# Issuing one input load from another engine's queue, and reordering the products around a weight fold

## The chip, the cores and the metric

The kernel runs on one core of one Trainium2 chip. The metric is the device time of one execution in microseconds (us), and a program's time is the median of its runs. A core has TensorE (PE, with its weight loads shown as PEld), VectorE (DVE), ScalarE (ACT), GpSimd (POOL), SyncE (SP, which here only issues DMAs) and 16 DMA engines. In this kernel TensorE's products go to PSUM, and ACT and DVE copy them from there to SBUF.

## The reference

```python
h  = x + A(layernorm(x))        # x: 2048 tokens x 640, bfloat16
h2 = h + B(layernorm(h))        # B: (gelu(x @ w_gate) * (x @ w_up)) @ w_down, 640 -> 1536 -> 640
# A: 32 heads of 20 columns
q, k, v = split(x @ wqkv)
phi(q)  = [softmax(q @ w_phi), softmax(-(q @ w_phi))]      # per head, 40 features
phi(k)  = the same of k
kv, z   = sum over tokens of phi(k) outer v,  sum of phi(k)
A(x)    = (phi(q) @ kv) / (phi(q) . z + 1e-6) @ wo
```

The attention is linear, so keys and values of all 2048 tokens must have been reduced to `kv` before any query can be finished.

## The kernel before, in words

Tokens are worked on in 16 tiles of 128 (`t` = 0 to 15), 640 columns each; the 640 rows of a weight are 5 blocks of 128 (`c`, or `d` for the blocks that a fold makes). `x_sb[b]` holds four tiles of x.

**Stages.** First each tile is normalized, transposed into `LN1T`, and multiplied by `Wv` (a v product, 10 matmuls of 320 columns) and by the folded key weight `Wk2` (a k product, also 10). This stage is what the change touches. After it come the queries (`q_mm`), attention, and the feed-forward block with the long `gate_up` and `down` products.

**The fold.** `w_phi` is applied to the key weight and not to the keys. For each block `d`, `fold(WkT, Wk2, False, (d,))` (L232) multiplies the transposed block `WkT[:, :, d]` by a block-diagonal matrix `BD`: 6 matmuls into a PSUM tile `wa`, which is then copied to `Wk2[:, d]`. Blocks 0, 1, 3 and 4 are copied by ACT (L257), block 2 by DVE (L259). `WkT` comes from HBM as five transposing DMAs, one for each `d`, issued by SP at L203 ahead of everything that SP issues later. A k product of block `c` needs `Wk2[:, c]`, so `k_part(t, c, ...)` (L326) can do some blocks of a tile before the other folds are made; `k_tile(t)` (L331) adds block 4 where a tile was begun that way (tiles 0 and 1), and runs the two exponentials on ACT (L340).

**PSUM.** All products share four PSUM tiles (`gtile`, L111, and the transposes' `tp`, L162), given out in rotation: a product can begin when the tile given out four places earlier has been read by ACT or DVE. So the order of calls also sets who waits for which copy.

**Order.** Nothing is reordered by a scheduler: each engine runs its instructions in the order of the program text. The text between L439 and L489 is an order written by hand, with halves of v products (`v_part`, L306), statistics (`ln_st`, L275, on DVE, with its `between` call inside), normalizations (`ln_ap`, L279), TensorE transposes (`ln_tp`, L286) and copies of v (`v_ev`, L315, on ACT). From tile 4 on the normalized tiles are transposed by DMAs that SP issues (L167).

**Loads of x.** Tiles 0 to 5 are loaded by SP at L189 to L198, ahead of the transposes of `WkT`. Tiles 6 and 7 are loaded by SP at L470, behind these transposes in SP's order, and read first by the statistics of L488. A DMA issue uses one of eight semaphores in rotation, and waits until the load eight issues earlier has landed; for L470 that is the load of tile 3 (L196). The one load that ACT issues before the change is that of `w_phi` (L191).

Of the kernel before, what the change touches and what calls it, by code (L numbers as in the profile page):

```python
# [17 lines left out]
def kernel(  # L18
# [12 lines left out]
    nc = tc.nc  # L31
# [41 lines left out]
    x_v = A_x.rearrange("b (p t) d -> p (b t) d", t=NT)  # L73
# [11 lines left out]
    x_sb = [const.tile([P, 4, D], BF16, name=f"x_sb{b}") for b in range(NB)]  # L85
# [25 lines left out]
    def gtile(name):  # L111
        return psG.tile([P, 2, 512], F32, name=name, tag="G")
# [46 lines left out]
    def transpose_to(dst, src, on_pe, on_dve=False):  # L159

        if on_pe:
            tp = psG.tile([P, 16, P], BF16, name="tp", tag="G")  # L162
            for c in range(NC):
                nc.tensor.transpose(tp[:, c, :], src[:, c * P:(c + 1) * P], ident)  # L164
            (nc.vector.tensor_copy if on_dve else nc.scalar.copy)(dst, tp[:, 0:NC, :])  # L165
        else:
            nc.sync.dma_start_transpose(dst, src)  # L167
# [9 lines left out]
    Wk2 = p1.tile([P, NC, D], BF16, name="Wk2")  # L177
# [5 lines left out]
    WkT = fp.tile([P, NC, D], BF16, name="WkT")  # L183
# [42 lines left out]
    def warm(*cols):  # L226
        for n in cols:
            nc.tensor.matmul(wu[:, 0, 0:n], lhsT=ones[:, 0:P], rhs=ones[:, 0:n], start=True, stop=True)
# [3 lines left out]
    def fold(WT, W2, quarters, ds=range(NC)):  # L232


        n, w = 1, HD
        runs = []
        for c in range(NC):
            lo, hi = H0[c] * Dh, (H0[c] + NH[c]) * Dh
            for r in range(2 * n):
                a, b = max(lo, r * w), min(hi, (r + 1) * w)  # L240
                if a < b:
                    runs.append((r // n, r, c, a, b))
        runs.sort()
        for d in ds:
            wa = gtile("wa")
            wr = wa.rearrange("p u (q x) -> p (u q) x", q=n)
            for i, (u, r, c, a, b) in enumerate(runs):
                nc.tensor.matmul(wr[:, r, a - r * w:b - r * w], lhsT=WT[:, c, d * P:(d + 1) * P],  # L248
                                 rhs=BD[:, c].rearrange("p a b -> p (a b)")[:, a - H0[c] * Dh:b - H0[c] * Dh],
                                 start=(i == 0 or runs[i - 1][0] != u),  # L250
                                 stop=(i + 1 == len(runs) or runs[i + 1][0] != u), skip_group_check=True)
            dst, src = W2[:, d, :].rearrange("p (u f) -> p u f", u=2), wr[:, :, 0:w]
            if quarters:
                dst = W2[:, d, :].rearrange("p (c u m f) -> p u m c f", c=NC, u=2, m=2)
                src = src.rearrange("p u (m c f) -> p u m c f", m=2, c=NC)
            if d in (QA if quarters else KA):
                nc.scalar.copy(dst, src)  # L257
            else:
                nc.vector.tensor_copy(dst, src)  # L259
# [19 lines left out]
    def ln_ap(t, on_act=False, on_pe=False):  # L279
        ln = (ln_act if on_act else ln_dve)(p1, "1", *lnp[t])  # L280
        if on_pe:
            lnp[t] = ln
        else:
            transpose_to(LN1T[t // 4][:, :, t % 4 * P:(t % 4 + 1) * P], ln, False)

    def ln_tp(t, on_dve=False):  # L286
        transpose_to(LN1T[t // 4][:, :, t % 4 * P:(t % 4 + 1) * P], lnp[t], True, on_dve)
# [5 lines left out]
    def proj(ps, t, W, us=(0, 1), cs=None):  # L293
        order = [(u, c) for u in us for c in range(NC)] if cs is None else [(u, c) for c in cs for u in us]
        for u, c in order:
            nc.tensor.matmul(ps[:, u, 0:HD], lhsT=lnT(t, c), rhs=W[:, c, u * HD:(u + 1) * HD],  # L296
                             start=(c == 0), stop=(c == NC - 1))
# [3 lines left out]
    def v_mm(t, us=(0, 1)):  # L301
        if 0 in us:
            pv[t] = gtile("pv")
        proj(pv[t], t, Wv, us)

    def v_part(t, *cs):  # L306

        if 0 in cs:
            pv[t] = gtile("pv")
        for c in cs:  # L310
            for u in range(2):
                nc.tensor.matmul(pv[t][:, u, 0:HD], lhsT=lnT(t, c), rhs=Wv[:, c, u * HD:(u + 1) * HD],  # L312
                                 start=(c == 0), stop=(c == NC - 1))

    def v_ev(t):  # L315
        nc.scalar.activation(vS[t % NV][:, :, 1:VC].rearrange("p (u h) f -> p u h f", u=2),
                             pv[t][:, :, 0:HD].rearrange("p u (h f) -> p u h f", f=Dh), ACTF.Copy,
                             scale=lnp[t][2] if t in CT else 1.0)
# [7 lines left out]
    def k_part(t, *cs):  # L326
        if 0 in cs:
            pks[t] = gtile("pk")
        proj(pks[t], t, Wk2, cs=cs)

    def k_tile(t):  # L331
        if t in pks:
            pk = pks[t]
            k_part(t, NC - 1)
        else:
            pk = gtile("pk")
            proj(pk, t, Wk2)
        Ek[t] = ev.tile([P, 2, D], BF16, name="E", bufs=10)
        for s in range(2):
            nc.scalar.activation(Ek[t][:, s, :].rearrange("p (u f) -> p u f", u=2), pk[:, :, 0:HD],  # L340
                                 ACTF.Exp, scale=((lnp[t][2], nrstd[t]) if t in CT else (1.0, -1.0))[s])
# [61 lines left out]
    def st_act(t, i):  # L403

        xt, v = x_sb[0][:, t, :], va[t]
        if i == 0:
            nc.scalar.activation(sqa, xt, ACTF.Identity, scale=-1.0 / D, accum_out=v[:, 0:1])
        else:
            nc.scalar.activation(sqa, xt, ACTF.Square, bias=v[:, 0:1], accum_out=v[:, 1:2])
            nc.gpsimd.tensor_scalar(v[:, 2:3], v[:, 1:2], 1.0 / D, EPS, op0=ALU.mult, op1=ALU.add)  # L410
            nc.gpsimd.tensor_tensor(v[:, 3:4], v[:, 2:3], nhalf[:, 0:1], op=ALU.pow)
            nc.gpsimd.tensor_scalar(nrstd[t], v[:, 3:4], -1.0, None, op0=ALU.mult)
            lnp[t] = xt, None, v[:, 3:4], None
# [16 lines left out]
    def bd(c0, c1):  # L430

        n = c1 - c0
        nc.vector.tensor_tensor(BD[:, c0:c1], wphi[:, c0:c1, None, :].to_broadcast([P, n, 8, Dh]),
                                hmask[:, c0:c1, :, None].to_broadcast([P, n, 8, Dh]), ALU.mult)
# [9 lines left out]
    ln_st(2, act=False, log=True)  # L444
    bd(0, NC)
    st_act(1, 1)
    warm(*[P] * 4)
    v_part(0, 0, 1)
    v_part(1, 0, 1)
# [17 lines left out]
                                op0=ALU.mult, op1=ALU.add)  # L467
    ln_st(4, act=False, between=lambda: ln_ap(3, on_pe=True))
    ln_tp(3, True)
    nc.sync.dma_start(x_sb[1][:, 2:4, :], x_v[:, 6:8, :])  # L470
    v_ev(2)
    fold(WkT, Wk2, False, (0,))
    fold(WkT, Wk2, False, (1,))
    ln_st(5, act=False, between=lambda: ln_ap(4))
    nc.sync.dma_start(x_sb[2][:, 0:2, :], x_v[:, 8:10, :])
    fold(WkT, Wk2, False, (2,))
    v_mm(3)
    v_ev(3)
    fold(WkT, Wk2, False, (3,))
    k_part(0, 0, 1, 2)  # L480
    k_part(1, 0)
    fold(WkT, Wk2, False, (4,))
    k_part(1, 1, 2)
    k_part(0, 3)
    k_part(1, 3)
    ln_ap(5)
    nc.sync.dma_start(x_sb[2][:, 2:4, :], x_v[:, 10:12, :])
    ln_st(6)  # L488
# [5 lines left out]
    for t in range(NT):  # L494
        if t == T3:
            kvp = gtile("kvp")[:, 0, 0:2 * QF].rearrange("p (s f) -> p s f", s=2)
        late = t in (1, 2, 3, 4)
        if 0 < t < NT - 6 and not late:
            ln_ap(t + 6, on_act=True)
        k_tile(t)  # L500
        if t == 0:
            ln_ap(6)
            nc.sync.dma_start(x_sb[3][:, 0:2, :], x_v[:, 12:14, :])
        if t in FQ:
            fold(WqT, Wq2, True, [i for i, f in enumerate(FQ) if f == t])
        for i in KVG.get(t, ()):
            kv_tile(i)
        for j in range(len(QT)):
            if t == QT[j]:
                q_mm(j)  # L510
                q_exp(j)
                if j == 0:
                    nc.gpsimd.tensor_copy(Wg[:, 0, 0:1], Eq[j][:, 0, 1, 0:1])
                for i in KVQ.get(j, ()):
                    kv_tile(i)
        if 0 < t < NT - 3:
            v_mm(t + 3)
        if late:
            ln_ap(t + 6, on_act=True)
        if t == 1:  # L520
            nc.sync.dma_start(x_sb[3][:, 2:4, :], x_v[:, 14:16, :])
        if 0 < t < NT - 3:
            v_ev(t + 3)
        for i in ST.get(t, ()):
            ln_st(i, i + 1)
        k_norm(t)
        load_T(WqT, 0, *[i for i, f in enumerate(LQ) if f == t])
        if t == 10:
            transpose_to(LN1T[0][:, :, P:2 * P], ln_a(1), False)
        if t == 13:  # L530
            ln_ap(0, on_act=True)
        if t == 8:
            for z in KT:
                nc.gpsimd.memset(z, 0.0)
        if t == 5:
            nc.sync.dma_start(Wo, wo_v)
# [401 lines left out]
```

## Time and profile before

| what | value |
|---|---|
| runs before | 271.77, 272.64, 272.80 us; median 272.64 |
| the profiled execution | 272.35 us |
| its span, first to last instruction | 270.6 us, so 1.75 us lie around it |
| TensorE busy | 266.1 us, 98% of the span |
| VectorE, ScalarE, GpSimd busy | 173.9, 138.6, 101.2 us |
| granted TensorE clock | 1.0 |
| HBM traffic | 47 GB/s over the span |

Times of instructions count from the start of the span. A matmul's row gives its start and the modelled time until its result is out; matmuls are pipelined, so ten of 320 columns that start 0.136 us apart take 1.36 us of TensorE's time although their row says 1.52. A bracket at the end of a row of the timeline is the idle time of the engine before it, and what ended it. The row of a DMA issue tells how long the issuing engine was at it; the landing of its data is another number.

### The profile page before, as it was taken

How to read it: one execution, taken by the hardware profiler on the slowest of the kernel's cores; microseconds unless marked ns; L12 is line 12 of the kernel's file. 1: busy time of each engine (PE TensorE's matmuls, PEld its weight loads, DVE VectorE, ACT ScalarE, POOL GpSimd, SP SyncE). 2: the span in 40 equal slices, each digit the busy share in tenths (PEclk: the TensorE clock that was granted, in tenths of full speed). 3: DMA queues.
4: the chain of work that ended last, by engine and by line, in shares of the span. 5: the costliest groups of instructions: out<-in, count | busy, mean ns of one | idle time of the engine just before them, and what ended most of it. 6: DMA issues, size and time to landing. Idle time of an engine off the chain costs nothing.

```text
span 270.6 us, 7029 instructions
## 1 busy us (share of the span) xinstructions
PE 266.1 (98%) x2857; PEld 172.0 (64%) x2857; DVE 173.9 (64%) x347; ACT 138.6 (51%) x249; POOL 101.2 (37%) x238
## 2 busy tenths in 40 slices
PE   8999999999999999999999999999999999999995
PEld 6777777765455887788755455775555476444574
DVE  5789999996877767876566783568673332333322
ACT  5779997877789675245541356421544300322100
POOL 5448898887002335376211564014661100000000
DMA  6987489213864442432301222203222101000011
GB/s 187 206 199 169 81 210 96 46 37 85 326 201 112 157 101 55 68 78 50 51 27 51 48 50 48 50 3 75 76 46 51 24 24 51 24 0 0 4 48 48
DMA packets 45264, 22.10 MB, mean 82 GB/s; under 512 B 37808, under 2 KB 43184, under 8 KB 45232
## 3 DMA queue, kind: packets, MB, share of 16 engines
q1 hardware_dynamic: 44576, 21.64, 33.5%
q8 instruction: 22, 0.36, 0.6%
q10 hardware_dynamic: 656, 0.03, 0.2%
q14 instruction: 10, 0.08, 0.1%
HBM read 10.18 MB, written 2.62 MB: 47 GB/s over the span
## 4 chain that ended last, share of the span: by engine, by line
PE 96%; DMA 2%; SPq 0%; DVE 0%; issue 0%
PE gu L768 39%; PE pd L790 19%; PE pq L396 8%; PE pk L296 8%; PE po L708 8%; PE pv L296 7%; DMA Wv<-in_A_wqkv_dram 2%; PE kvp L374 2%; PE pv L312 2%; PE ab L619 1%; PE wa L248 1%; PE ab L586 1%; PE tp L164 0%; SPq L193 0%; SPq L190 0%; SPq L189 0%
## 5 line engine op out<-in xcount | busy, mean ns | idle before, releaser
L771 ACT ACTIVATE g<-gu 128x512 bf16<-128x512 f32 (+1 forms) x60 | 30.4, 510 | 74.0 <-PE gu L768 73.2
L774 DVE TENSOR_TENSOR GT<-gu,g 128x512 bf16<-128x512 f32 (+1 forms) x60 | 34.3, 579 | 46.8 <-PE gu L768 38.6
L768 PE MATMUL gu<-LN2T,Wg 128*128 128x512 bf16 (+1 forms) x300 | 61.8, 337 | 0.0
L768 PE MATMUL gu<-LN2T,Wu 128*128 128x512 bf16 (+1 forms) x300 | 61.8, 336 | 0.0
L790 PE MATMUL pd<-Wd,GT 128*128 128x320 bf16 (+4 forms) x396 | 53.9, 295 | 0.0
L790 PEld LDWEIGHTS <-GT 128*128 128x128 bf16 x396 | 37.6, 98 | 14.5 <-DVE GT L774 0.2
L768 PEld LDWEIGHTS <-Wu 128*128 128x128 bf16 x300 | 29.4, 98 | 22.6
L768 PEld LDWEIGHTS <-Wg 128*128 128x128 bf16 x300 | 29.1, 98 | 21.2
L296 PEld LDWEIGHTS <-LN1T 128*128 128x128 bf16 x290 | 28.0, 98 | 10.4
L355 POOL TENSOR_TENSOR E<-E,rs 128x640 bf16<-128x640 bf16 x25 | 31.7, 1295 | 4.4 <-DVE rs L351 2.8
L792 DVE TENSOR_TENSOR y<-pd,x_sb 128x320 bf16<-128x320 f32 (+4 forms) x33 | 15.8, 480 | 24.1 <-PE pd L790 24.1
L708 PE MATMUL po<-Wo,oT 128*128 128x320 bf16 x160 | 24.5, 299 | 0.0
L296 PE MATMUL pk<-Wk,LN1T 128*128 128x320 bf16 x160 | 24.4, 299 | 0.0
L396 PE MATMUL pq<-LN1T,Wq 128*128 128x512 bf16 x100 | 22.9, 379 | 0.0
L347 DVE TENSOR_REDUCE sk<-E 128x64 f32<-128x1280 bf16 x16 | 22.9, 1430 | 0.0
L401 ACT ACTIVATE Eq<-pq 128x1024 bf16<-128x1024 f32 (+1 forms) x26 | 19.9, 831 | 2.8 <-PE pq L396 2.7
L340 ACT ACTIVATE E<-pk 128x640 bf16<-128x640 f32 x28 | 19.1, 769 | 3.0 <-PE pk L296 3.0
L708 PEld LDWEIGHTS <-oT 128*128 128x128 bf16 x160 | 15.6, 98 | 7.3 <-ACT oT L165 0.2
L296 PE MATMUL pv<-Wv,LN1T 128*128 128x320 bf16 x130 | 19.8, 299 | 0.0
L151 ACT ACTIVATE ln<-x_sb,v,rstd 128x640 bf16<-128x640 bf16 x14 | 12.9, 920 | 13.0 <-POOL v L747 12.9
L396 PEld LDWEIGHTS <-Wq 128*128 128x128 bf16 x100 | 9.4, 98 | 10.3
L683 DVE TENSOR_TENSOR tt<-AB,w 128x1280 bf16<-128x1280 f32 x10 | 15.1, 1505 | 0.4 <-POOL w L676 0.3
(120 smaller groups left out, 291.4 us busy)
## 6 DMA issues: line engine op xcount, KB each, us to landing
out_dram<-y SPq DMA_DIRECT2D x15, 160.0 KB, 1.8
x_sb<-in_A_x_dram SPq DMA_DIRECT2D x6, 320.0 KB, 3.3
Wd<-in_B_w_down_dram SPq DMA_DIRECT2D x1, 1440.0 KB, 6.8
Wg<-in_B_w_gate_dram SPq DMA_DIRECT2D x1, 1152.0 KB, 7.3
Wu<-in_B_w_up_dram SPq DMA_DIRECT2D x1, 1152.0 KB, 5.6
Wo<-in_A_wo_dram SPq DMA_DIRECT2D x1, 800.0 KB, 5.0
Wg<-in_B_w_gate_dram SPq DMA_DIRECT2D x1, 768.0 KB
Wu<-in_B_w_up_dram SPq DMA_DIRECT2D x1, 768.0 KB, 9.1
```

What stands on the lines that cost most here:

```text
L296: nc.tensor.matmul(ps[:, u, 0:HD], lhsT=lnT(t, c), rhs=W[:, c, u * HD:(u + 1) * HD], start=(c == 0), stop=(c == NC - 1))
L340: nc.scalar.activation(Ek[t][:, s, :].rearrange("p (u f) -> p u f", u=2), pk[:, :, 0:HD], ACTF.Exp, scale=((lnp[t][2], nrstd[t]) if t in C ...
L347: nc.vector.reduce_sum(sk, Ek[t].rearrange("p s (h f) -> p (s h) f", f=Dh), axis=AX.X)
L355: eng.tensor_tensor(e, e, rs[:, s * H:(s + 1) * H, None].to_broadcast([P, H, Dh]), ALU.mult)
L396: nc.tensor.matmul(pqs[j][:, i, :], lhsT=Wq2[:, kc, c * P:(c + 1) * P], rhs=LN1T[b][:, kc, :], start=(kc == 0), stop=(kc == NC - 1))
L401: nc.scalar.activation(Eq[j][:, :, s, :], pqs[j][:, 0:len(QG[j])], ACTF.Exp, scale=(1.0, -1.0)[s])
L708: nc.tensor.matmul(pos[u], lhsT=st[t][:, c, :], rhs=Wo[:, c, u * HD:(u + 1) * HD], start=(c == 0), stop=(c == NC - 1))
L768: nc.tensor.matmul(gu[i][:, 0:n], lhsT=W[:, c, f * P:(f + 1) * P], rhs=LN2T[b][:, c, a0:a1], start=(c == 0), stop=(c == NC - 1))
L771: nc.scalar.activation(g[:, 0:n], gu[0][:, 0:n], ACTF.Gelu_apprx_tanh)
L774: nc.vector.tensor_tensor(st[b, "g", f][:, a0:a1], gu[1][:, 0:n], g[:, 0:n], ALU.mult)
L790: nc.tensor.matmul(pd[:, 0:f1 - f0], lhsT=st[b, "g", f][:, tl * P:(tl + 1) * P], rhs=Wd[:, f, f0:f1], start=(f == 0), stop=(f == NF - 1), ...
L792: nc.vector.tensor_tensor(y[:, f0:f1], pd[:, 0:f1 - f0], x_sb[b][:, tl, f0:f1], ALU.add)
```

## The change

The load of x tiles 6 and 7 is taken from SP (L470) and given to ACT, in the text right after the second half of tile 1's statistics (L446). SP has one load less between the transposes of `WkT` and the first transpose of a normalized tile.

The other edits change the order of TensorE's work, with the copies that belong to it:

- the fold of block 2 moves from before the v product of tile 3 to after it;
- ahead of the fold of block 4 there is only block 0 of tile 0's k product and block 0 of tile 1's (before: blocks 0, 1, 2 of tile 0 and block 0 of tile 1);
- after that fold, tile 0's blocks 1, 2, 3 and (in `k_tile`) 4 are done together, and tile 1's blocks 1, 2, 3 follow after tile 0's `k_tile`, ahead of tile 1's.

No matmul, copy or load is added or taken away.

```diff
     bd(0, NC)
     st_act(1, 1)
+    nc.scalar.dma_start(x_sb[1][:, 2:4, :], x_v[:, 6:8, :])
     warm(*[P] * 4)
...
     ln_tp(3, True)
-    nc.sync.dma_start(x_sb[1][:, 2:4, :], x_v[:, 6:8, :])
     v_ev(2)
     fold(WkT, Wk2, False, (0,))
     fold(WkT, Wk2, False, (1,))
     ln_st(5, act=False, between=lambda: ln_ap(4))
     nc.sync.dma_start(x_sb[2][:, 0:2, :], x_v[:, 8:10, :])
-    fold(WkT, Wk2, False, (2,))
     v_mm(3)
     v_ev(3)
+    fold(WkT, Wk2, False, (2,))
     fold(WkT, Wk2, False, (3,))
-    k_part(0, 0, 1, 2)
+    k_part(0, 0)
     k_part(1, 0)
     fold(WkT, Wk2, False, (4,))
-    k_part(1, 1, 2)
-    k_part(0, 3)
-    k_part(1, 3)
+    k_part(0, 1, 2, 3)
     ln_ap(5)
...
         k_tile(t)
         if t == 0:
+            k_part(1, 1, 2, 3)
             ln_ap(6)
```

## The prediction

> **What bounds the kernel now.** I read the chain that ended last first, then TensorE's list of waits, then the timeline of each engine around the change. The page's chain:
>
> ```profile
> PE 96%; DMA 2%; SPq 0%; DVE 0%; issue 0%
> ```
>
> TensorE carries 96% of it. Everything that it waited for in 270.6 us, from its list of waits:
>
> ```profile
> PE pv L312 <- DMA Wv<-in_A_wqkv_dram: 0.9, 1, 0.9
> PE wu L228 <- PEq L922: 0.8, 1, 0.8
> ```
>
> Both lie before 7.41 us, ahead of everything that the change moves. From there TensorE goes without a listed wait to the last product. Its timeline around the change:
>
> ```profile
> 11.76 0.45 PE L164 MATMUL tp<-ident,ln 128*128 128x128 bf16 x5
> 12.04 1.15 PE L248 MATMUL wa<-BD,WkT 128*128 128x140 bf16 x18
> 13.02 1.52 PE L296 MATMUL pv<-Wv,LN1T 128*128 128x320 bf16 x10
> 14.38 0.48 PE L248 MATMUL wa<-BD,WkT 128*128 128x140 bf16 x6
> 14.70 1.25 PE L296 MATMUL pk<-Wk,LN1T 128*128 128x320 bf16 x8
> 15.78 0.48 PE L248 MATMUL wa<-BD,WkT 128*128 128x140 bf16 x6
> 16.10 1.79 PE L296 MATMUL pk<-Wk,LN1T 128*128 128x320 bf16 x12
> 17.73 0.43 PE L296 MATMUL pv<-Wv,LN1T 128*128 128x320 bf16 x2
> ```
>
> From start to start: 10 matmuls of 320 columns take 1.36 us (13.02 to 14.38), so 0.136 each; a fold takes 0.32 (14.38 to 14.70). Three folds take 0.98 (12.04 to 13.02) where 3 x 0.32 = 0.96 would do: the third waited about 0.04 for a PSUM tile. That is all the slack there is. So **the change can't win time by removing a wait here; it can only add waits** or leave the time alone. The question is how tightly the new order fits the copies and the loads:
>
> ```profile
> 11.96 0.70 ACT L316 ACTIVATE vS<-pv 128x640 bf16<-128x640 f32 x1
> 12.56 1.29 ACT L257 CAST Wk<-wa 128x640 bf16<-128x640 f32 x2
> 14.58 0.70 ACT L316 ACTIVATE vS<-pv 128x640 bf16<-128x640 f32 x1 [0.74 <-PE pv L296]
> 15.18 0.69 ACT L257 CAST Wk<-wa 128x640 bf16<-128x640 f32 x1
> 16.30 0.69 ACT L257 CAST Wk<-wa 128x640 bf16<-128x640 f32 x1 [0.43 <-PE wa L248]
> 17.66 0.79 ACT L340 ACTIVATE E<-pk,rstdc 128x640 bf16<-128x640 f32 x1 [0.67 <-PE pk L296]
> ```
>
> ```profile
> 12.26 0.48 DVE L165 COPY LN1T<-tp 128x640 bf16<-128x640 bf16 x1
> 14.35 0.77 DVE L259 CAST Wk<-wa 128x640 bf16<-128x640 f32 x1
> ```
>
> A copy of a product into SBUF takes 0.70 on ACT and 0.77 on DVE. It starts 0.04 after the product's last result is out (the row of the v product ends at 14.54, ACT starts at 14.58), and TensorE goes on about 0.05 after a copy has ended (ACT's copy ends at 12.66, the third fold starts at 12.71).
>
> **The reorder, step by step.** The same 48 matmuls lie between the second fold's end (12.67) and tile 4's v product (17.73): 5.02 us of work and the 0.04 of waiting. In the new order, with who holds the PSUM tile that each product takes over:
>
> - v of tile 3 comes right after the second fold. It takes the tile that `v_ev(2)` frees at 12.66, and reads `LN1T` of tile 3, which DVE has copied at 12.26 + 0.48 = 12.74. Start 12.80, a wait of 0.13. End 14.16.
> - folds 2 and 3: 14.16 to 14.79. Their PSUM tiles are free by 13.85.
> - k of tile 0, block 0: to 15.07, no wait (`Wk2` block 0 has long been copied).
> - k of tile 1, block 0 takes over tile 3's v. Its last result is out at 14.33, ACT copies from 14.36 to 15.06. Start 15.11, a wait of 0.05. End 15.38.
> - fold 4 takes over fold 2, which DVE copies: out at 14.64, copy 14.68 to 15.45. Start 15.50, a wait of 0.12. End 15.82. (Before, fold 4 took over tile 3's v, copied at 15.28, and started at 15.78.)
> - k of tile 0, blocks 1, 2, 3: 6 x 0.136 = 0.82, to 16.63. Block 3's copy ends at 14.96 + 0.69 = 15.65, in time.
> - k of tile 0, block 4 needs fold 4's copy: out at 15.98, copy 16.02 to 16.71. Start 16.76, a wait of 0.13.
> - the last two matmuls of tile 0 and eight of tile 1: 1.36 us. Tile 4's v starts at **18.12**, against 17.73.
>
> Sum: 0.13 + 0.05 + 0.12 + 0.13 = 0.43 of waits against 0.04 before, so **+0.4 us**. The old order covered fold 4's copy with four more matmuls of k, and fold 2's copy with a whole v product.
>
> Is it given back? Tile 0's exponentials start near 17.23 and not at 17.66, so ACT gets ahead of TensorE by that plus the 0.4. But TensorE waits for no exponential afterwards, and being early is worth nothing to an engine that isn't awaited. So I give nothing back; bounds of that are 0 and -0.4.
>
> **The load, step by step.** SP loses an issue of 0.58 at 12.36. Its next issue waits for DVE's tile 4 (13.81 against 12.94) and stays where it is. The data:
>
> ```profile
> 16.27 0.89 DVE L121 BATCH_NORM_STATS2 stats<-x_sb 128x6 f32<-128x320 bf16 x2 [0.42 <-DMA x_sb<-in_A_x_dram]
> ```
>
> DVE waited 0.42 for tiles 6 and 7. That goes. What is late next is DVE's own queue: its copy of fold 2 ends 0.33 later than before, which takes most of it back. Tile 6's v product is 7 us away (23.16), so this reaches no one: 0.
>
> What ACT pays: an issue of 0.46 (that of L191) to 0.58 (SP's L470). It waits for tile 3's load, landed at 8.59, and is done by 9.17; ACT is idle until 9.78 (1.63 of idle before it), so 0, with 0.6 of cover left. Queued behind it are tile 0's v copy at 9.78, then L131, L132, tile 1's and tile 2's v copies: they free the tiles for the folds.
>
> What the DMA engines pay: 320 KB move beside the transposes of `WkT`. Landings, from the five issues and the DMA view of each: 4.63 + 5.9 = 10.5, 6.57 + 4.7 = 11.3, 7.88 + 4.2 = 12.1, 9.72 + 3.5 = 13.2, 11.04 + 4.5 = 15.5. The new order needs them at 12.36 less 0.05 (block 1), 14.16 (block 2), 14.48 (block 3), 15.50 (block 4): margins of 1.0, 2.0, 1.2 and 0. Block 4 landed late with the load of tiles 6 and 7 right behind it; now that load is gone from there. In the best half microsecond of that load, 14.5 to 15.0, the engines moved 369 GB/s, so 320 KB cost 0.89 us: inside the margins of blocks 1 to 3. From below: 9.0 to 9.5 shows a DMA share of 0.06 and 11.0 to 11.5 one of 0.47, so part of it falls into empty time, and block 4 could come earlier, which TensorE's copies wouldn't let it use. From above: where copies and the first transposes met, 8.5 to 9.5, the two half microseconds moved 122 and 26 GB/s instead of some 250, a loss of 0.7 us; 0.89 + 0.7 = 1.6 late leaves block 1 0.6 too late. I take 0, as the nearest row (369 GB/s) has it, and keep 0.6.
>
> The Trainium skill ("DMA: Bandwidth & Descriptors", Issuing engines are not separate DMA queues) says that DMAs of different issuing engines run on the same 16 DMA engines and interleave, and that issuing from several saves only issue time. No row here shows an ACT load beside transposes; by that rule the load is paid by the blocks of `WkT`, the first rival.
>
> **Sum:** 272.35 + 0.4 = 272.75 for the profiled execution. That lies 0.29 below the median of the runs, so against the median 272.64 + 0.4 = **273.0**.
>
> **Rivals.**
>
> 1. *The load holds up `WkT`* (slower). Its place is fold 1, needed 0.3 earlier than any other block. It decides from a delay of 1.0 us on. With the 1.6 above: 272.64 + 0.4 + 0.6 = 273.6; at twice the 0.7 of loss, 2.3 late, 1.3 of stall, 274.3. For it: the stretch 8.5 to 9.5. Against it: the idle shares, and a margin larger than 0.89. Chance 0.20, a third of it past 274.0.
> 2. *ACT is held at the issue* (slower). SP's third transpose is at its issue from 7.88 to 9.68, 1.80 us. If ACT's issue had to wait for it, it would end at 9.68 + 0.58 = 10.26; tile 1's v copy then ends at 12.17 and fold 0 starts 0.18 late, of which 0.05 remains at the v product: 273.1. If it waited for the next one too (11.00), ACT resumes 1.8 late and about 1.3 of it reaches TensorE: 274.3. Against it: the issues of L191 on ACT and L189 on SP both start at 0.79 and take 0.46 and 0.40, so they ran abreast. Chance 0.08 for the large form. The Trainium skill ("Perfetto Trace Analysis", DMA Instruction — HWDGE) says that an issuing engine locks the descriptor generator for exclusive use; the row at 0.79 shows no such wait.
> 3. *No new wait shows*: copies a little earlier than I have them, or the lead of ACT is used. 272.64 - 0.04 = 272.6. Chance 0.12.
> 4. *Faster by over 0.5%*, under 271.28: no wait is long enough, so only from a luckier start (the runs before span 271.77 to 272.80). Chance 0.05.
>
> My forecast, +0.2 to +0.7, has the remaining 0.55. Half a per cent, 1.36 us, is about what a measurement of this kernel can tell from no change. Under 271.28: 0.05. Above 274.0: 0.07 of the first rival, 0.06 of the second, 0.02 of the forecast's scatter, 0.15. Between: 0.80. The range goes from the fastest run before with a small cost, 271.9, to the first rival's far end, 274.2.
>
> **What would show it.** Right: tile 4's first v product near 18.1, fold 4 near 15.5, tile 0's first exponential near 17.2, ACT's DMA issue between 8.6 and 9.2, still no large wait of TensorE. Wrong: a wait of TensorE on a load of `WkT` ahead of fold 1 or 4; tile 0's v copy on ACT after 9.8; or tile 4's v product at 17.8 or earlier. A gain of a microsecond would mean that TensorE's dense rows hide a wait that I can't see.

## The result and the profile after

The changed kernel takes 273.62 us (median of 13 runs, 272.48 to 275.51), the kernel before 271.79 (13 runs, 271.38 to 272.80): a ratio of 1.0068, with a 95% interval of 1.0051 to 1.0086. That is 1.83 us more, where +0.4 was forecast. The 13 runs of before, which include the prediction's three, have a lower median than these three alone (272.64). The execution profiled for the prediction had also started late: its first v product waited for `Wv` until 7.41, where the profiles of the other versions begin it between 6.4 and 6.8. Ratios and intervals, here and below, leave out a run that is more than 1.5% above the fastest of its kernel (only 276.11 of e1) and are taken over the runs, so they need not be the quotient of the two medians.

The profile that came with the result is of the slowest of the 13 executions, 275.51 us with a span of 273.8. Its chain:

```profile
PE 93%; DMA 3%; SPq 2%; DVE 1%; issue 0%
PE gu L767 38%; PE pd L789 19%; PE pk L296 8%; PE pq L396 8%; PE po L707 8%; PE pv L296 6%; DMA WkT<-in_A_wqkv_dram 3%; PE kvp L374 2%; PE ab L618 1%; PE wa L248 1%; SPq L203 1%; PE ab L585 1%; DVE stats L121 0%; PE tp L164 0%; SPq L195 0%
```

A load of `WkT` now carries 3% of the chain, about 7 us, where before none of its loads was on it. TensorE's list of waits in the same profile:

```profile
PE wa L248 <- DVE stats L121: 1.1, 1, 1.1
PE wu L228 <- PEq L921: 0.8, 1, 0.8
PE wa L248 <- DMA WkT<-in_A_wqkv_dram: 0.7, 1, 0.7
```

Two folds wait, for 0.7 and 1.1 us. The first row names DVE, whose statistics also end at 16.82; but a fold reads no statistics, and block 4 of `WkT` landed at 16.82 (issued at 10.33, 6.5 to landing), so this fold, which started at 16.86, waited for the block.

A second profile of the changed kernel, label e11 below, is of an execution of 273.67 us, close to the median, and I read the wait times from it. TensorE's timeline there:

```profile
11.16 0.79 PE L248 MATMUL wa<-BD,WkT 128*128 128x140 bf16 x12
11.91 1.53 PE L296 MATMUL pv<-Wv,LN1T 128*128 128x320 bf16 x10
14.03 0.90 PE L248 MATMUL wa<-BD,WkT 128*128 128x140 bf16 x12 [0.59 <-DMA WkT<-in_A_wqkv_dram]
14.76 0.71 PE L296 MATMUL pk<-Wk,LN1T 128*128 128x320 bf16 x4
16.50 0.49 PE L248 MATMUL wa<-BD,WkT 128*128 128x140 bf16 x6 [1.03 <-DMA WkT<-in_A_wqkv_dram]
16.83 2.46 PE L296 MATMUL pk<-Wk,LN1T 128*128 128x320 bf16 x16
19.13 1.52 PE L296 MATMUL pv<-Wv,LN1T 128*128 128x320 bf16 x10
```

From start to start, against the lengths that the prediction took from the rows before: the v product of tile 3 could have handed over at 11.91 + 1.36 = 13.27, and fold 2 starts at 14.03, 0.76 late. Four matmuls of k end at 14.76 + 0.54 = 15.30, and fold 4 starts at 16.50, 1.20 late. The rest of the waits is small: 0.12 ahead of the v product, 0.10 behind fold 2, 0.13 in the last k products. Sum 2.31, less the 0.04 of before: 2.3 us. The measured difference of this run to the median beside it (271.57) is 2.10.

### The profile page after: what moved, and what is told of

Its sections match the earlier page's. It is cut to its first block, busy times and chain, and to the rows that moved or that the text cites. A ratio compares the mean times of both kernels' runs of the same rounds, so it can differ in the third digit from the quotient of the medians.

```text
span 273.8 us, 7029 instructions
## 1 busy us (share of the span) xinstructions
PE 268.2 (98%) x2857; PEld 172.5 (63%) x2857; DVE 173.4 (63%) x347; ACT 139.1 (51%) x249; POOL 101.3 (37%) x238
## 4 chain that ended last, share of the span: by engine, by line
PE 93%; DMA 3%; SPq 2%; DVE 1%; issue 0%
PE gu L767 38%; PE pd L789 19%; PE pk L296 8%; PE pq L396 8%; PE po L707 8%; PE pv L296 6%; DMA WkT<-in_A_wqkv_dram 3%; PE kvp L374 2%; PE ab L618 1%; PE wa L248 1%; SPq L203 1%; PE ab L585 1%; DVE stats L121 0%; PE tp L164 0%; SPq L195 0%
## 5 line engine op out<-in xcount | busy, mean ns | idle before, releaser
L296 PEld LDWEIGHTS <-LN1T 128*128 128x128 bf16 x290 | 28.5, 100 | 11.3
L296 PE MATMUL pk<-Wk,LN1T 128*128 128x320 bf16 x160 | 25.7, 310 | 0.0
L340 ACT ACTIVATE E<-pk 128x640 bf16<-128x640 f32 x28 | 18.5, 729 | 2.9 <-PE pk L296 2.9
```

## The experiments

All times are medians, with the kernel before, run beside it on the same chip, after the word "against". From e2 on the diffs are against the changed kernel; `...` marks where lines are left out.

### The load alone, and the order alone

e1 has the early load on ACT with the order of before:

```diff
     st_act(1, 1)
+    nc.scalar.dma_start(x_sb[1][:, 2:4, :], x_v[:, 6:8, :])
     warm(*[P] * 4)
...
-    nc.sync.dma_start(x_sb[1][:, 2:4, :], x_v[:, 6:8, :])
```

> The load of tiles 6 and 7 on ACT ahead of the later blocks of WkT, with the order of before. Theory M (the load and the transposes share the DMA engines and the transposes come late): blocks 2, 3 and 4 land 1.5 to 3 us later than before (12.1, 13.2 and 15.5); fold 2, which this order wants at 12.7, waits 1 to 2 us; the time is 1.2 to 2.2 us above before. Theory R (the loss comes from the new order, whose copies don't fit): within 0.3 us of before.

Measured: 273.77 against 271.66, 1.0068 (1.0043 to 1.0092). This order wants block 2 first, and TensorE's timeline shows it waiting there:

```profile
11.40 0.79 PE L248 MATMUL wa<-BD,WkT 128*128 128x140 bf16 x12
14.23 0.49 PE L248 MATMUL wa<-BD,WkT 128*128 128x140 bf16 x6 [2.04 <-DMA WkT<-in_A_wqkv_dram]
```

Block 2, issued by SP at 7.29, landed 6.9 us later, at 14.19. The load alone makes a loss as large as the whole change's. Theory R falls for the larger part. Fold 4 did not wait in this order: block 4 landed at 16.67 and fold 4 started at 17.32.

e2 has the other half, the new order with the load on SP at its old place:

```diff
     st_act(1, 1)
-    nc.scalar.dma_start(x_sb[1][:, 2:4, :], x_v[:, 6:8, :])
     warm(*[P] * 4)
...
     ln_tp(3, True)
+    nc.sync.dma_start(x_sb[1][:, 2:4, :], x_v[:, 6:8, :])
     v_ev(2)
```

> The new order of folds and k products, with the load of tiles 6 and 7 left on SP at its old place. Theory M: only the four short waits that the prediction summed, 0.2 to 0.6 us above before; fold 4 starts 2.8 us after the v product of tile 3, tile 4's v product 5.3 us after it. Theory R: 1.5 to 2 us above before, like the changed kernel.

Measured: 272.11 against 271.66, 1.0021 (1.0012 to 1.0029), +0.45 us. Its TensorE timeline:

```profile
11.33 0.79 PE L248 MATMUL wa<-BD,WkT 128*128 128x140 bf16 x12
12.08 1.53 PE L296 MATMUL pv<-Wv,LN1T 128*128 128x320 bf16 x10
13.45 0.79 PE L248 MATMUL wa<-BD,WkT 128*128 128x140 bf16 x12
14.08 0.76 PE L296 MATMUL pk<-Wk,LN1T 128*128 128x320 bf16 x4
14.84 0.49 PE L248 MATMUL wa<-BD,WkT 128*128 128x140 bf16 x6
15.16 2.46 PE L296 MATMUL pk<-Wk,LN1T 128*128 128x320 bf16 x16
17.46 0.71 PE L296 MATMUL pv<-Wv,LN1T 128*128 128x320 bf16 x4
```

No bracket stands there, because each wait is short, but the starts tell them: 11.33 + 0.63 = 11.96 and the v product at 12.08 (0.12); k at 14.08 + 0.54 = 14.62 and fold 4 at 14.84 (0.22 in two waits); sixteen k matmuls are 2.17, so 17.33, and tile 4's v at 17.46 (0.13). Sum 0.47, where 0.43 was predicted. At fold 4 two causes end together: DVE's copy of fold 2 at 14.78 and block 4's landing at 14.79.

The landing of block 2 tells the two kernels apart; the last column is us from issue to landing, and the issues started at 7.28 (e2) and 7.30 (e11). First e2, then the changed kernel (e11) with ACT's load beside it:

```profile
WkT<-in_A_wqkv_dram SPq DMA_TRANSPOSE x1, 4.1
```

```profile
x_sb<-in_A_x_dram ACTq DMA_DIRECT2D x1, 320.0 KB, 6.1
WkT<-in_A_wqkv_dram SPq DMA_TRANSPOSE x1, 6.7
```

The two losses don't add up (2.1 and 0.45, against 1.83), though e1's interval, 1.2 to 2.5 us, is wide. The new order asks for block 2 later by a v product, 1.36 us, and waits less for it (0.76 in e11 against e1's 2.04), but then it waits for block 4 too (1.20).

### Where the load is issued, and when

e3 issues it from ACT after the v copy of tile 2:

```diff
     st_act(1, 1)
-    nc.scalar.dma_start(x_sb[1][:, 2:4, :], x_v[:, 6:8, :])
...
     v_ev(2)
+    nc.scalar.dma_start(x_sb[1][:, 2:4, :], x_v[:, 6:8, :])
     fold(WkT, Wk2, False, (0,))
```

> The new order, and the load still issued by ACT, but after the v copy of tile 2, when SP has issued all five transposes. Theory M: the transposes are ahead on every DMA engine, so blocks 2, 3 and 4 land within 0.5 us of before; 0.2 to 0.7 us above before, as the new order alone. If the loss came from ACT as the issuing engine (its queue held, whatever the place): 1 us or more above before.

Measured: 273.22 against 271.66, 1.0048 (1.0026 to 1.0070); seven runs, three of them at 271.9 to 272.2 and four at 273.2 to 274.1. The expectation missed, because the place was not late enough: ACT reached it at 11.28, while SP was at the issue of block 4 (10.59 to 11.86). Blocks 2 and 3 landed 4.4 and 3.8 us after their issue (in e2 4.1 and 3.5); block 4 landed with the load, at 16.34 against 14.79. Fold 4 paid for it:

```profile
PE wa L248 <- DMA WkT<-in_A_wqkv_dram: 1.5, 1, 1.5
```

So the miss says the same as e1, of another block: what is moved beside the load comes late. e7 goes behind ACT's copies of folds 0 and 1:

```diff
     st_act(1, 1)
-    nc.scalar.dma_start(x_sb[1][:, 2:4, :], x_v[:, 6:8, :])
...
     fold(WkT, Wk2, False, (1,))
+    nc.scalar.dma_start(x_sb[1][:, 2:4, :], x_v[:, 6:8, :])
```

> The new order with the load on ACT after its copies of folds 0 and 1, so that its data comes when block 4 has been moved. If the loss of the changed kernel and of the load after the v copy of tile 2 is the mixing with transposes of W_k: 0.3 to 0.7 us above before, as the order alone (0.45). If it is ACT as issuing engine: 1 us or more.

Measured: 272.07 against 271.69, 1.0013 (1.0004 to 1.0021). That is the order alone, and block 4 landed at 14.83, as in e2 (14.79). ACT as the issuing engine is cleared.

e4 issues the load from SP between two transposes:

```diff
-    load_T(WkT, 1, *range(NC))
+    load_T(WkT, 1, 0, 1)
+    nc.sync.dma_start(x_sb[1][:, 2:4, :], x_v[:, 6:8, :])
+    load_T(WkT, 1, 2, 3, 4)
...
     st_act(1, 1)
-    nc.scalar.dma_start(x_sb[1][:, 2:4, :], x_v[:, 6:8, :])
```

> The new order, and the load issued by SP between the transposes of blocks 1 and 2: as many bytes ahead of blocks 2 to 4 as in the changed kernel, but in one queue and so not mixed packet by packet. If the loss is made by the mixing of two queues: blocks 2 to 4 land about 0.9 us later than before, margins of 2.0 and 1.2 us hide most of it, 0.3 to 1.0 us above before. If it is made by the bytes that stand ahead, or by each change from transposes to copies and back: 1.5 to 2 us above before, like the changed kernel.

Measured: 272.52 against 271.66, 1.0029 (1.0018 to 1.0039). The load landed at 11.33, 4.1 us after its issue at 7.28; ACT's, issued at 7.7 to 7.9, took 6.0 to 6.2. Block 2 landed at 12.5 and block 3 at 13.2. The same bytes ahead of the same blocks cost 0.4 us over the order alone when they stand in one queue, and 1.4 when they come from a second. Block 2 was in time; e4's list of waits has one on the blocks, fold 4's for block 4, of 0.8.

e10 takes e7's place for the load with the order of before.

> The order of before, with the load on ACT after its copies of folds 0 and 1, clear of the transposes of W_k: SP has one issue less, nothing else differs from before. If TensorE's dense order leaves nothing to win and the load costs only by its place: within 0.2 us of before. If one issue less on SP brings the later transposes of tiles forward in a way that counts: 0.3 us or more below before, and faster than both kernels.

Measured: 271.73 against 271.57, 1.0003 (0.9994 to 1.0012). Behind the transposes the load costs nothing, and having SP free of it wins nothing. No version beat the kernel before.

### Bytes, packets, or the moment

e5 makes the five blocks of W_k plain copies:

```diff
+    def load_P(WT, i):
+        for d in range(NC):
+            nc.sync.dma_start(WT[:, :, d * P:(d + 1) * P],
+                              A_wqkv[d * P:(d + 1) * P, i * D:(i + 1) * D].rearrange("p (c n) -> p c n", c=NC))
-    load_T(WkT, 1, *range(NC))
+    load_P(WkT, 1)
...
     nc.scalar.dma_start(x_sb[1][:, 2:4, :], x_v[:, 6:8, :])
+    load_P(WqT, 0)
```

> The changed kernel with the five blocks of W_k loaded by plain copies in packets of the same 256 bytes (not transposed, so the keys are computed from another matrix), and five more such copies of W_q right behind ACT's load, so that both queues have work at the same time; read is the rate while both queues move data, and the time of a packet of the ACT load, not the time of the kernel. In the changed kernel both queues together moved about 150 GB/s from 10.0 to 13.5 and a packet of 2560 bytes took about 0.27 us in place of 0.10. If any two queues that mix slow each other so: at most 180 GB/s, packets of 0.25 us or more. If it is the mixing of copies with transposes: 250 GB/s or more, packets of 0.10 to 0.15 us.

The table by half microseconds tells it; the last two columns are the DMA engines' busy share (over 1 where packets that start there end later) and GB/s. The changed kernel (e11), both queues at work:

```profile
10.00:10.50 0.50, 1.00 1.38 146
10.50:11.00 0.50, 1.00 0.91 129
11.00:11.50 0.50, 1.00 0.92 209
11.50:12.00 0.50, 1.00 1.23 220
12.00:12.50 0.50, 1.00 1.26 159
12.50:13.00 0.50, 1.00 1.51 87
13.00:13.50 0.50, 1.00 1.37 27
```

The plain copies (e5), both queues at work until the load landed at 12.54:

```profile
10.00:10.50 0.50, 1.00 1.08 252
10.50:11.00 0.50, 1.00 1.01 325
11.00:11.50 0.50, 1.00 1.08 294
11.50:12.00 0.50, 1.00 1.20 271
```

That is 140 GB/s on average over the 3.5 us and 176 from 10.00 to 12.00, busy all the while, against 285 from 10.00 to 12.00 here. In e2, where the load comes later, the engines moved 142 GB/s over the same 3.5 us at a mean share of 0.76: the early load added busy time and hardly any bytes. In the trace's records a packet of the load took 0.41 and 0.26 us on average in the first two stretches of the changed kernel, and 0.11 to 0.15 here. In this one execution two queues that mix copies with copies didn't slow each other so. The load of e5 was issued at 8.51, though, and the changed kernel's at 7.7 to 7.9; e5 doesn't hold the kind of traffic apart from the moment, to which e12 comes back.

e6 takes tile 6 alone early (the first diff), e9 half of the partitions of both tiles (the second):

```diff
-    nc.scalar.dma_start(x_sb[1][:, 2:4, :], x_v[:, 6:8, :])
+    nc.scalar.dma_start(x_sb[1][:, 2:3, :], x_v[:, 6:7, :])
...
     ln_tp(3, True)
+    nc.sync.dma_start(x_sb[1][:, 3:4, :], x_v[:, 7:8, :])
```

```diff
-    nc.scalar.dma_start(x_sb[1][:, 2:4, :], x_v[:, 6:8, :])
+    nc.scalar.dma_start(x_sb[1][0:64, 2:4, :], x_v[0:64, 6:8, :])
...
     ln_tp(3, True)
+    nc.sync.dma_start(x_sb[1][64:P, 2:4, :], x_v[64:P, 6:8, :])
```

> The changed kernel with tile 6 alone issued early by ACT and tile 7 by SP at the old place: half of the bytes in the mix. If the delay grows with the bytes that are mixed in: about half of the 1.3 us that the early load costs over the order alone, so 0.9 to 1.5 us above before. If the mere presence of a second queue (each change of kind) sets it: 1.6 to 2.1 us, like the changed kernel. If the margins swallow half a load: 0.4 to 0.7 us, like the order alone.

> The changed kernel with half of the partitions of both tiles issued early by ACT, the other half by SP at the old place: 160 KB early as in the half load, in packets of 2560 bytes. If the length of the packets makes the delay: 0.9 to 1.9 us above before, packets of the early load at 0.2 us or more. If it is the bytes: 0.3 to 0.8 us above before, like the half load.

Measured: e6 272.25 against 271.69, 1.0018 (1.0007 to 1.0029); e9 272.27 against 271.62, 1.0023 (1.0013 to 1.0034). Both are the order alone within their intervals: half of the load is free, in packets of either length, though it moves beside transposes.

e8 has the whole load early in two issues.

```diff
-    nc.scalar.dma_start(x_sb[1][:, 2:4, :], x_v[:, 6:8, :])
+    nc.scalar.dma_start(x_sb[1][:, 2:3, :], x_v[:, 6:7, :])
+    nc.scalar.dma_start(x_sb[1][:, 3:4, :], x_v[:, 7:8, :])
```

> The changed kernel with the early load cut in two issues of ACT, one for each tile: all 320 KB early, in packets of 1280 bytes as in the half load, which cost nothing over the order alone. If the length of the packets that are mixed between the transposes makes the delay: 0.3 to 0.8 us above before, packets at 0.06 us each, blocks 2 and 3 within 0.7 us of the half load's (11.8 and 12.7). If it is the bytes, which take more than the free time between the transposes: 1.5 to 2.1 us above before, like the changed kernel, block 2 after 13.5.

Measured: 272.63 against 271.62, 1.0036 (1.0021 to 1.0050), between the two expectations; block 2 landed at 13.07, in time, and the wait was fold 4's for block 4 (1.0). Neither reading is excluded by it.

The half loads had also been issued later than the whole one, at 8.2 and 8.4 and not at 7.7 to 7.9, because they got another of the eight semaphores. e12 delays the whole load as much:

```diff
     st_act(1, 1)
+    nc.scalar.copy(sqa, x_sb[0][:, 1, :])
     nc.scalar.dma_start(x_sb[1][:, 2:4, :], x_v[:, 6:8, :])
```

> The changed kernel with one more copy of tile 1 (0.7 us, its result is not used) on ACT ahead of the load, so that the whole load is issued at about 8.5, as late as the two half loads were (8.2 and 8.4, because they got another semaphore), and not at 7.7 to 7.9. If the bytes make the delay: 1.3 to 2.1 us above before, block 2 after 13.0. If it was the moment at which the load meets the transposes: 0.3 to 0.8 us above before, block 2 before 12.8, as with the half loads.

Measured: 272.76 against 271.72, 1.0048 (1.0028 to 1.0068), seven runs from 272.37 to 274.26. Again between. But its profile, of the 272.37, shows a whole load that did no harm:

```profile
10.00:10.50 0.50, 1.00 1.23 333
10.50:11.00 0.50, 1.00 1.04 415
11.00:11.50 0.50, 1.00 1.18 292
```

All 320 KB went through in these 1.5 us, 347 GB/s with the transposes' data, packets at 0.10 to 0.11 us; block 2 landed at 12.04 and block 3 at 12.75. So the bytes alone don't make the delay. Neither does a mix of copies and transposes by itself, so what e5 seemed to show of the kind of traffic stays open. In the profiles the moment goes with the harm: where ACT's issue started at 7.6 to 7.9 (the changed kernel twice, e1, e8), block 2 landed at 13.1 to 14.3; where it started at 8.2 to 8.4 (e6, e9, e12), at 11.7 to 12.1. These are single executions, and e12's slower runs say that the later moment doesn't always spare it. It is a collision that comes in some executions and not in others: e1 ran from 271.68, no loss at all, to 276.11, and e3 in two groups.

### A second look at the changed kernel

> The changed kernel once more, for a second profile: the first one was of its slowest execution, with TensorE at half clock from 17.4 to 20.2. If that is a consequence that comes in some executions only: 273.3 to 274.0 us, clock 1.00 throughout, waits of 1 to 2 us in all on blocks 2 and 4 of W_k. If half clock belongs to the change: again 0.99 and over 274.5.

Measured: 273.67, clock 1.00 throughout. In the first profile the clock column (the third from the end here) tells where the rest of its 275.51 went:

```profile
14.00:16.00 2.00, 1.48 (x16) 0.93 (x16) 1.15 (x3) 1.02 (x2) 0.56 (x2) 1.00 1.62 151
16.00:17.40 1.40, 0.54 (x6) 0.54 (x7) 1.36 (x6) 0.00 (x0) 0.17 (x1) 0.78 0.86 209
17.40:20.20 2.80, 2.80 (x14) 1.64 (x12) 2.10 (x7) 1.08 (x2) 2.07 (x6) 0.50 1.16 213
20.20:22.00 1.80, 1.80 (x15) 1.30 (x14) 1.56 (x5) 1.80 (x4) 0.74 (x2) 1.00 0.88 173
```

The 0.78 of the second row is 0.6 us at half clock (1.4 x 0.22 / 0.5), so half clock lasted 3.4 us, from 16.8 to 20.2. TensorE worked from 16.86 on, so about 1.7 us are lost. Two of the 13 runs and three of e1's twelve show a mean clock of 0.993 or 0.994, and all but one of these are above 275; no run of the kernel before beside the experiments is below 0.998. So it comes in some executions of the versions with long waits, and is not what makes the median; that the waits bring it is argued from this.

## Why the prediction was right or wrong

**Right: the bound, and the new order.** TensorE had no wait to lose, so the change could only add some. The order alone costs 0.45 (0.33 to 0.79 by its interval) where 0.4 was worked out, and the terms came where they were put: 0.12 for 0.13, 0.22 for 0.05 + 0.12, 0.13 for 0.13. Nothing was given back later. One reading was off without effect: ACT is at tile 3's v copy until 15.06, so block 3's copy ends about 0.1 later than the 15.65 given, still ahead of its use.

**Wrong: the term of the load.** The failing step is "I take 0, as the nearest row (369 GB/s) has it". That row is of copies following each other in one queue, with no transposes between them. Beside transposes from another queue the engines moved 140 GB/s for 3.5 us, and the load's term was 1.4 us (1.83 less 0.45) and not 0. The stretch from 8.5 to 9.5, which I kept as the far end, was the nearer row: copies meeting transposes. That the delay would stay inside the margins was wrong for blocks 2 and 4.

**The first rival was what happened, in the wrong place.** I put it at fold 1 as the narrowest margin, although my own list gives block 4 a margin of 0. Block 1 came in time in the profiles of the changed kernel (11.0 and 11.3), 0.5 to 0.7 later than in e2 (10.5). A wait ahead of fold 4 was among the signs of being wrong, and it came; no sign named the one ahead of fold 2. Block 2 used up its margin of 2.0 (landing 14.0 against 11.4 in e2, the start being the same) and block 4, which had none, came at 16.5 against 14.8. I had put block 4's late landing down to the load right behind it and had it gaining when that load left, and the gain never came: block 4 took 4.5 us from issue to landing before, and 4.7 in e7 and in e12's profile, where the load is elsewhere. The rival's price of 273.6 is 1.0 above the median it stood on, where 1.83 was measured; that the number agrees with 273.62 is chance, and two waits made it, not the one that I worked out.

**The second rival didn't come.** ACT's issue took 0.35 to 0.36 us beside SP's transposes, and tile 0's v copy waited for its product as before.

**The range held in part by luck.** The forecast stood on a median of 272.64; the 13 runs have 271.79. On that base it would have read 272.2, and 1.4 us would have been missing. The chance of 0.15 for more than half a per cent was too low: the trace showed no row of an ACT load beside transposes, and I let an absent row count as a margin.

**What stays open.** What decides in an execution whether the load collides with the transposes is not settled: the half loads and e12's profiled run passed freely beside them, e8 and e12's other runs lie between. Kind of traffic, number of bytes and moment are not held apart.

Block 4's lateness has a part of its own, which is not the load's. In every profile with transposed blocks but e3's it landed 2.0 to 2.4 us after block 3, in e2 as well (12.51 and 14.79; 15 of its 16 shares were there by 13.26). By these times block 3's delay (14.4 in e11, 12.5 in e2) was passed on to block 4, and so to fold 4. In e4 it landed 2.1 us after block 3 although the load was long done, and the DMA engines moved nothing in between:

```profile
13.00:13.50 0.50, 1.00 0.46 100
13.50:14.00 0.50, 1.00 0.00 0
14.00:14.50 0.50, 1.00 1.14 182
```

In the first of these stretches the DMA view shows one packet of the instruction queue, 16 KB, which held its engine for 0.98 us; the same stands in the changed kernel between 14.0 and 15.0. In the kernel before it came at 13.31, when block 4 was almost through: 15 of its 16 shares landed by 14.03, the sixteenth at 15.54. That the fetch holds up the transposes is argued from these times; no run took it away.

## What to carry to other kernels

A load that gets a queue of its own doesn't get DMA engines of its own: look at what is being moved at the moment when it will arrive, and if these are transposes that TensorE waits for soon, keep the load behind them (e10: nothing lost), or in their queue (e4: 0.4), or small (e6, e9), where alone and early it cost 2.1 (e1). Where TensorE has no waits, an earlier transfer has nothing to win; ask first who waits for it. A margin taken from one profile is worth the row that it was priced by, and a row of the same kind of traffic, however ugly, is nearer than a clean one.

## What the runs showed of the hardware that I had not expected

In the changed kernel's second profile copies from ACT's queue and transposes from SP's moved 140 GB/s together for 3.5 us. With SP's blocks as plain copies in packets of the same 256 bytes both queues moved 285, and in e12's profile the same two kinds as in the changed kernel passed at 347. The Trainium skill ("DMA: Bandwidth & Descriptors", Issuing engines are not separate DMA queues) has the two queues interleave on the same engines; the blocks that came late agree with that.

TensorE's clock fell to half for 3.4 us after waits of 0.7 and 1.1 us within 3.3 us in one profiled execution, and stayed at 1.00 in e1's profile with a single wait of 2.04 and in e11 with 0.59 and 1.03. The Trainium skill ("TensorE: Matmul & The Clock Gate", Part 1: The HAM clock gate) has it fall after an idle window of about 3.4 us that runs freely; that it came in some executions only fits a window that runs freely, but no wait here was nearly as long.
